# Grouping the state update and the 64-row steps of an mLSTM and feed-forward kernel

## The chip, the cores and the metric

The kernel runs on one core of a Trainium2 chip. The metric is the device time of one execution in microseconds (us); less is better. The profiles come from the hardware profiler.

## The reference

Two blocks follow one another. The first is an mLSTM cell with 4 batches, 8 heads, 768 steps and head size 40. The second is a feed-forward layer on the 3072 tokens that come out, with width 320 and 2048 hidden units.

```python
for t in range(S):
    m_new = np.maximum(f_gate[:, :, t] + m, i_gate[:, :, t])
    f_stab = np.exp(f_gate[:, :, t] + m - m_new)
    i_stab = np.exp(i_gate[:, :, t] - m_new)
    m = m_new
    C = f_stab[..., None, None] * C + i_stab[..., None, None] * np.einsum('bhd,bhe->bhde', vt, kt)
    n = f_stab[..., None] * n + i_stab[..., None] * kt
    h_tilde = np.einsum('bhde,bhe->bhd', C, qt)
    denom = np.maximum(np.abs(np.einsum('bhd,bhd->bh', n, qt)[:, :, None]), 1.0)
    y[:, :, t] = h_tilde / denom / (1.0 + np.exp(-o_gate[:, :, t]))
x = y.transpose(0, 2, 1, 3).reshape(B * S, H * D)
h = x @ w_in
out = (h / (1.0 + np.exp(-1.702 * h))) @ w_out
```

## The kernel before

The sequence is cut into six windows of 128 steps, `w` = 0 to 5. Inside a window the recurrence is computed as attention: scores of q and k, weighted by the gates and masked, times v, plus what the state from earlier windows gives. Everything is float32; one matmul of the program is two matmuls (and two weight loads) in the profile. TensorE (PE) executes them in order. It is used in several array forms: all 128 rows and columns; two halves of 64 rows side by side (scores `p_s`, and the last 64 of the 320 inputs of the up-projection, `w_in_x`, L423); two halves of 64 columns side by side (`p_o`, `p_i`, and the state update `p_c`); and 32 rows for the decay product (L282).

A window goes through these stages.

- `gates(w)` on VectorE (DVE) computes the running gates. From window 1 on its `dec` is a 32-row operand, from which `columns` makes the decay of the states by a matmul with `half`.
- `attention(w)` is a list of eight steps: `columns`, then for step s the functions `seam` of batch s-3, `values` of batch s-2, `scores` of batch s-1 and `weights` of batch s. GpSimd (POOL) masks the weights (L329) and copies 64 columns of y (L372). `values` reads v (`v_st`, with a column of ones at its end) and the state.
- `up(w, j)` is the up-projection of the pairs j and j+1 of the 16 blocks of 128 hidden units, for all four batches at once: `full(j)` is 8 matmuls of 512 columns, `rest(j)` 4 of the 64-row form. Its order is full, rest, rest, full. `gelu` on ScalarE (ACT) takes the result out of PSUM.
- `carry(w, b)` makes the new states of batch b: POOL scales v into `vw` (L386) and multiplies the old state by its decay (L396), PE multiplies k by `vw` (L391), and DVE adds (L400; a copy, L402, in window 0). Carries 0 and 1 follow the first `up` of a window, carries 2 and 3 the second.
- `down` (window 0) and `down_fast` (windows 1 to 5) are the down-projection. The eight attention steps of the next window are spread between its blocks, at the places in `stops`. `hidden_sums` on DVE prepares operands for `down_fast`, and `weight_sums` does so once, in window 1.

Window 0 also converts the weights, which arrive as 64-bit numbers: `convert(n)` does piece n with two operations on ACT and four on DVE (L224 to L229). Pieces 3 and 4 are converted within the first `up` of window 0, pieces 18 and 19 between blocks of its down-projection, each ahead of the `transposes` of batch 2 and 3 of window 1 on DVE. `transposes` turns k and q (L294), and `scores` waits for it.

PSUM has two pools of four banks: `ps_m` for up- and down-projection, `ps_a` for all else. Loads and stores are issued by SyncE (SP) in the program's order; `spread` sends the gate rows, which `gates` has written to DRAM (`m_row`), to all 128 partitions.

Of the kernel before, what the change touches and what calls it, by code (L numbers as in the profile page):

```python
# [8 lines left out]
FP = mybir.dt.float32  # L9
# [25 lines left out]
def kernel(  # L35
# [156 lines left out]
        V.tensor_scalar(out=pick[j * BH:(j + 1) * BH, :], in0=ident[0:BH, 0:BH], scalar1=-1.0, scalar2=None,  # L192
                        op0=OP.mult)

    half = const.tile([BH, 2, 64], FP, name="half")
    par = const.tile([BH, 2], FP, name="par")
    pair = const.tile([BH, BH // 2], FP, name="pair")
    V.tensor_reduce(out=par, in_=ident[0:BH, 0:BH].rearrange("p (j two) -> p two j", two=2), axis=AX.X, op=OP.add)
    V.tensor_reduce(out=pair, in_=ident[0:BH, 0:BH].rearrange("p (j two) -> p j two", two=2), axis=AX.X, op=OP.add)
    V.tensor_copy(out=half, in_=par.unsqueeze(2).to_broadcast([BH, 2, 64]))  # L200
    for t in (k_st, q_st):
        G.memset(t[:, :, D:DP], 0.0)

# [28 lines left out]
    def gates(w):  # L232
        m = m_at[w]
        f_run = gate.tile([BH, L], FP, bufs=1, name="f_run")
        m_run = gate.tile([BH, L], FP, bufs=1, name="m_run")
        st = stacked[w] = gate.tile([3 * BH, L], FP, name="st")
        V.tensor_tensor_scan(out=f_run, data0=ones, data1=f_sb[w], initial=0.0, op0=OP.mult, op1=OP.add)
        a = st[0:BH, :]
        V.tensor_tensor(out=a, in0=i_sb[w], in1=f_run, op=OP.subtract)
        if w == 0:  # L240
            room = work.tile([L, H, D1], FP, tag="u", name="room").rearrange("p h d -> p (h d)")
            neg, part = room[0:BH, 0:L], room.bitcast(BF)[0:BH, 2 * L:3 * L]
            V.tensor_tensor(out=neg, in0=f_run, in1=i_sb[w], op=OP.subtract)
            for j in range(3):
                G.tensor_copy(out=part, in_=neg)
                G.tensor_copy(out=a3[j * BH:(j + 1) * BH, :], in_=part)
                if j < 2:
                    G.tensor_tensor(out=neg, in0=neg, in1=part, op=OP.subtract)
        V.tensor_tensor_scan(out=m_run, data0=ones, data1=a, initial=m, op0=OP.mult, op1=OP.max)
        if w == 0:  # L250

            room = work.tile([L, H, D1], FP, tag="u", name="room").rearrange("p h d -> p (h d)")
            left, part = room[0:BH, 0:L], room.bitcast(BF)[0:BH, 2 * L:3 * L]
            for j in range(3):
                rest = left if j else m_run
                V.tensor_copy(out=part, in_=rest)
                V.tensor_copy(out=m3[j * BH:(j + 1) * BH, :], in_=part)
                if j < 2:
                    V.tensor_tensor(out=left, in0=rest, in1=part, op=OP.subtract)
        else:  # L260
            m_row[w] = rows.tile([BH, L], FP, name="m_row")
            nc.sync.dma_start(out=m_row[w], in_=m_run)
        end = m_run[:, L - 1:L]
        if w + 1 < NW:
            m_at[w + 1] = gate.tile([BH, 1], FP, name="m_end")
            V.tensor_tensor(out=m_at[w + 1], in0=f_run[:, L - 1:L], in1=end, op=OP.add)

        V.tensor_scalar(out=st[BH:2 * BH, :], in0=m_run, scalar1=m, scalar2=None, op0=OP.subtract)
        V.tensor_scalar(out=st[2 * BH:3 * BH, :], in0=a, scalar1=end, scalar2=-1.0, op0=OP.subtract, op1=OP.mult)
        if 0 < w < NW - 1:  # L270
            dec[w] = gate.tile([BH, BH // 2], FP, name="dec")
            both = gate.tile([BH, 1], FP, name="both")
            V.tensor_tensor(out=both, in0=m, in1=end, op=OP.subtract)
            V.tensor_scalar(out=dec[w], in0=pair, scalar1=both, scalar2=None, op0=OP.mult)

    def columns(w):
        pt = ps_a.tile([L, 3 * BH + BH // 2], FP, tag="a", name="p_cols")
# [101 lines left out]
            T.transpose(px[:, c, :], ys[w, b][:, c * 128:(c + 1) * 128], ident)  # L379
        A.copy(out=xT[w][:, :, b, :], in_=px)  # L380

    def carry(w, b):
        hs = slice(b * H, (b + 1) * H)
        vw = work.tile([L, H, D1], FP, tag="vw", name="vw")
        e = cols[w][:, 2 * BH + b * H:2 * BH + (b + 1) * H].unsqueeze(2).to_broadcast([L, H, D1])
        G.tensor_tensor(out=vw, in0=v_st[:, hs, :], in1=e, op=OP.mult)  # L386
        pc = ps_a.tile([128, NP, D1], FP, tag="a", name="p_c")
        for p in range(NP):
            for i in range(2):
                h = 2 * p + i  # L390
                T.matmul(pc[i * 64:i * 64 + D, p, :], k_st[:, b * H + h, 0:D], vw[:, h, :], start=True, stop=True)  # L391
        ps = slice(b * NP, (b + 1) * NP)
        if w:
            d = cols[w][:, 3 * BH + b * NP:3 * BH + (b + 1) * NP].unsqueeze(2).to_broadcast([128, NP, 2 * D1])
            old = state[:, ps].rearrange("p j a b -> p j (a b)")
            G.tensor_tensor(out=old, in0=old, in1=d, op=OP.mult)  # L396
        for i in range(2):
            r = slice(i * 64, i * 64 + D)
            if w:
                V.tensor_tensor(out=state[r, ps, i, :], in0=pc[r], in1=state[r, ps, i, :], op=OP.add)  # L400
            else:
                V.tensor_copy(out=state[r, ps, i, :], in_=pc[r])  # L402


    def up(w, j, between=None):

        x = xT[w].rearrange("p c b t -> p c (b t)")
        ph = {}  # L410
        ts = slice(0, W)

        def full(j, first):
            for c in range(2):
                for i in range(2):
                    f = 2 * j + i
                    T.matmul(ph[j][i][:, ts], w_in_sb[:, c, f * 128:(f + 1) * 128], x[:, c, ts],  # L417
                             start=(first and c == 0), stop=(not first and c == 1))

        def rest(j, first):  # L420
            for i in range(2):
                r = slice(i * 64, i * 64 + 64)
                T.matmul(ph[j][i][:, ts], w_in_x[r, j, :], x[r, 2, ts], start=first, stop=not first)  # L423

        def gelu(j):
            g = gs[w, j] = gp.tile([128, 2, W], FP, tag="g", name="g")
            for i in range(2):
                A.activation(out=g[:, i, :], in_=ph[j][i], func=AF.Gelu_apprx_sigmoid)  # L428

        if between:  # L430
            for k in (j, j + 1):
                ph[k] = [ps_m.tile([128, W], FP, tag="m", name="p_h") for _ in range(2)]
            ts = slice(0, W // 2)
            full(j, True)
            between[0]()
            rest(j, False)
            rest(j + 1, True)
            between[1]()
            full(j + 1, False)
            between[2]()  # L440
            ts = slice(W // 2, W)
        for j, first in ((j, True), (j + 1, False)):
            if j not in ph:
                ph[j] = [ps_m.tile([128, W], FP, tag="m", name="p_h") for _ in range(2)]
            if first:
                full(j, True)
            rest(j, not first)
            if not first:
                full(j, False)
            gelu(j)  # L450

    def down(w, b, n):
        if n == 0:
# [79 lines left out]
    def attention(w):  # L533
        steps = [[(columns, w)]]
        for s in range(B + 3):
            step = []
            for lag, f in ((3, seam), (2, values), (1, scores), (0, weights)):
                if 0 <= s - lag < B:
                    step.append((f, w, s - lag))
            steps.append(step)  # L540
        return steps

# [47 lines left out]
    def weights_in(n):  # L590
        done, ahead = beside.get(n, ((), ()))
        for p in done:
            convert(p)
        for p in ahead:
            fetch(p)

    for w in range(NW):
        more = w + 1 < NW
        for j in range(NF // 2):
            if j % 2 == 0:  # L600
                if w == 0 and j == 0:
                    up(w, j, (lambda: values(0, 2), lambda: values(0, 3),
                              lambda: (seam(0, 2), seam(0, 3), convert(3), convert(4))))
                    weights_in(0)
                else:
                    if w == 0:
                        weights_in(j // 2)
                    up(w, j)
            if j == 0 and more:
                load(w + 1, "o")  # L610
            if w == 0 and j == 0:
# [5 lines left out]
            if more:  # L617
                if w and j == 0:
                    gates(w + 1)
                if j == 4:  # L620
                    if w == 0:
                        load_blocks(1, 1)
                    load(w + 1, "v")
                    if w:
                        spread(w + 1)
                if j == (4 if w else 6):
                    load(w + 1, "k")
                if j < B:
                    carry(w, j)
                if w == 0 and j == 0:  # L630
                    G.memset(q_bl, 0.0)
                if w and 4 <= j < 6:
                    transposes(w + 1, 2 * j - 8)
                    transposes(w + 1, 2 * j - 7)
# [56 lines left out]
```

## Time and profile before

| | |
|---|---|
| median of 7 runs | 516.41 us (516.39 to 518.82) |
| profiled execution | 516.43 us, span 514.7 us |
| PE busy | 506.3 us, 98% of the span |
| DVE, ACT, POOL busy | 268.5, 169.2, 71.1 us |
| up-projection matmuls, 128 rows (L417) | 400, 175.6 us |
| up-projection matmuls, 64 rows (L423) | 200, 48.0 us |
| state matmuls p_c (L391) | 320, 8.1 us |
| POOL vw (L386), state decay (L396) | 20 of 0.829 us, 16 of 0.893 us (mean) |
| granted TensorE clock | 1.00 |

Busy time of an engine is the union of its instructions, so matmuls that overlap count once. A matmul's recorded length includes its way through the array (0.6 us for 512 columns); the pace is read from the starts. An engine's idle time costs something only where PE waits for it. In the timeline, rows of one kind that follow without a gap are merged into one.

### The profile page before, as it was taken

How to read it: one execution, taken by the hardware profiler on the slowest of the kernel's cores; microseconds unless marked ns; L12 is line 12 of the kernel's file. 1: busy time of each engine (PE TensorE's matmuls, PEld its weight loads, DVE VectorE, ACT ScalarE, POOL GpSimd, SP SyncE). 2: the span in 40 equal slices, each digit the busy share in tenths (PEclk: the TensorE clock that was granted, in tenths of full speed). 3: DMA queues.
4: the chain of work that ended last, by engine and by line, in shares of the span. 5: the costliest groups of instructions: out<-in, count | busy, mean ns of one | idle time of the engine just before them, and what ended most of it. 6: DMA issues, size and time to landing. Idle time of an engine off the chain costs nothing.

```text
span 514.7 us, 9527 instructions
## 1 busy us (share of the span) xinstructions
PE 506.3 (98%) x3838; PEld 351.3 (68%) x3838; DVE 268.5 (52%) x597; ACT 169.2 (33%) x373; POOL 71.1 (14%) x104
## 2 busy tenths in 40 slices
PE   8899999999999999999999999999999999999997
PEld 4774367774449996447999445999543899744797
DVE  6879984963865543175454146455137545203511
ACT  5557675303128202215421122720212730122100
POOL 7231000112301102200212200110120111000000
PEclk9999999999999999999999999999999999999999
DMA  9999789005897404686100495400485000000000
GB/s 148 180 302 293 118 222 184 5 33 80 103 254 81 59 3 78 124 165 69 28 14 20 83 244 62 44 27 1 79 210 56 0 29 1 27 0 0 1 27 25
DMA packets 175691, 44.80 MB, mean 87 GB/s; under 512 B 164352, under 2 KB 170528, under 8 KB 175648
## 3 DMA queue, kind: packets, MB, share of 16 engines
q1 hardware_dynamic: 175648, 44.21, 45.7%
q8 instruction: 30, 0.49, 0.4%
q14 instruction: 13, 0.11, 0.1%
HBM read 40.17 MB, written 4.01 MB: 86 GB/s over the span
## 4 chain that ended last, share of the span: by engine, by line
PE 94%; DVE 2%; POOL 1%; ACT 1%; issue 1%; DVEq 0%; POOLq 0%
PE p_h L417 33%; PE p_out L511 30%; PE p_h L423 9%; PE p_out L457 7%; PE p_o L350 5%; PE p_s L339 4%; PE p_i L356 2%; PE p_c L391 1%; PE p_x L379 1%; DVE wt L341 0%; ACT xT L380 0%; POOL k_bl L555 0%; DVE pick L192 0%; PE p_cols L282 0%; POOL state L554 0%
## 5 line engine op out<-in xcount | busy, mean ns | idle before, releaser
L417 PE MATMUL p_h<-xT,w_in_sb 128*128 128x512 f32 (+1 forms) x400 | 175.6, 585 | 1.2 <-ACT xT L380 1.2
L417 PEld LDWEIGHTS p_h<-xT,w_in_sb 128*128 128x128 f32 x400 | 72.7, 190 | 90.4 <-issue 86.9
L428 ACT ACTIVATE g<-p_h 128x512 f32<-128x512 f32 x96 | 54.6, 596 | 155.8 <-PE p_h L423 91.1
L511 PE MATMUL p_out<-w_out_sb,g 128*128 128x160 f32 x480 | 71.3, 302 | 0.0
L511 PEld LDWEIGHTS p_out<-w_out_sb,g 128*128 128x128 f32 x480 | 66.8, 190 | 3.7 <-issue 2.4
L516 DVE TENSOR_TENSOR o_sb<-o_sb,p_out 128x160 f32<-128x160 f32 x70 | 21.5, 319 | 72.9 <-PE p_out L511 72.3
L380 ACT COPY xT<-p_x 128x384 f32<-128x384 f32 x24 | 11.4, 480 | 134.8 <-PE p_x L379 134.8
L329 POOL TENSOR_SCALAR_AFFINE_SELECT wt<-wt 128x1024 f32<-128x1024 f32 x24 | 26.6, 1108 | 174.7 <-ACT wt L326 142.8
L326 ACT ACTIVATE wt<-wt,cols 128x128 f32<-128x128 f32 x160 | 48.3, 390 | 0.0
L423 PE MATMUL p_h<-xT,w_in_x 64*128 64x512 f32 (+1 forms) x200 | 48.0, 598 | 0.2 <-DVE w_in_x L229 0.2
L511 PE MATMUL p_out<-t,s 128*128 128x160 f32 x320 | 47.5, 301 | 0.0
L511 PEld LDWEIGHTS p_out<-t,s 128*128 128x128 f32 x320 | 44.3, 190 | 0.6
L495 DVE TENSOR_TENSOR s<-g 128x512 f32<-128x512 f32 x20 | 13.9, 693 | 54.0 <-ACT g L428 54.0
L400 DVE TENSOR_TENSOR state<-p_c,state 40x164 f32<-40x164 f32 x32 | 10.4, 326 | 53.9 <-PE p_c L391 53.5
L423 PEld LDWEIGHTS p_h<-xT,w_in_x 64*128 64x128 f32 x200 | 17.2, 186 | 29.0 <-issue 27.4
L457 PE MATMUL p_out<-w_out_sb,g 128*128 128x320 f32 x128 | 36.2, 437 | 0.0
L341 DVE TENSOR_TENSOR wt<-p_s,wt 128x512 f32<-128x512 f32 x48 | 30.8, 684 | 8.3 <-PE p_s L339 5.5
L457 PEld LDWEIGHTS p_out<-w_out_sb,g 128*128 128x128 f32 x128 | 23.8, 190 | 10.1 <-issue 0.5
L350 PEld LDWEIGHTS p_o<-v_st,wt 128*64 128x64 f32 x768 | 24.3, 138 | 6.4 <-issue 4.7
L350 PE MATMUL p_o<-v_st,wt 128*64 128x41 f32 x768 | 27.2, 231 | 1.4 <-DVE wt L341 1.4
L339 PE MATMUL p_s<-qT,kT 40*128 40x128 f32 x384 | 27.9, 285 | 0.5 <-DVE wt L341 0.4
L339 PEld LDWEIGHTS p_s<-qT,kT 40*128 40x128 f32 x384 | 23.3, 187 | 3.9 <-issue 1.3
(114 smaller groups left out, 507.9 us busy)
## 6 DMA issues: line engine op xcount, KB each, us to landing
wt<-m_row SPq DMA_DIRECT2D x20, 512.0 KB, 6.4
bits<-in_moe_w_in_dram SPq DMA_DIRECT2D x8, 512.0 KB, 5.6
out_dram<-o_sb SPq DMA_DIRECT2D x24, 160.0 KB, 1.8
eo<-in_o_gate_dram SPq DMA_DIRECT2D x5, 640.0 KB, 5.7
v_st<-in_v_dram SPq DMA_DIRECT2D x5, 640.0 KB, 5.9
k_st<-in_k_dram SPq DMA_DIRECT2D x5, 640.0 KB, 8.2
bits<-in_moe_w_out_dram SPq DMA_DIRECT2D x8, 320.0 KB, 4.3
k_bl<-in_k_dram SPq DMA_DIRECT2D x40, 64.0 KB, 2.7
```

What stands on the lines that cost most here:

```text
L326: A.activation(out=x[:, h, :], in_=x[:, h, :], func=AF.Exp, scale=-1.0, bias=cols[w][:, b * H + h:b * H + h + 1])
L329: G.affine_select(out=x, in_=x, compare_op=OP.is_ge, fill=0.0, base=0, pattern=[[0, H], [1, L]], channel_multiplier=-1)
L339: T.matmul(pw[i][:, p, :], kT[w, b][r, p, :], qT[w, b][r, p, :], start=True, stop=True)
L341: V.tensor_tensor(out=wt[w, b][:, :, i, :], in0=pw[i], in1=wt[w, b][:, :, i, :], op=OP.mult)
L350: T.matmul(po[t, h, :], wt[w, b][:, p, i, t], v_st[:, b * H + h, :], start=True, stop=True)
L417: T.matmul(ph[j][i][:, ts], w_in_sb[:, c, f * 128:(f + 1) * 128], x[:, c, ts], start=(first and c == 0), stop=(not first and c == 1))
L423: T.matmul(ph[j][i][:, ts], w_in_x[r, j, :], x[r, 2, ts], start=first, stop=not first)
L428: A.activation(out=g[:, i, :], in_=ph[j][i], func=AF.Gelu_apprx_sigmoid)
L457: T.matmul(po, gs[w, f // 2][:, f % 2, b * L:(b + 1) * L], w_out_sb[:, f, :], start=(f == 0), stop=(f == NF - 1))
L495: V.tensor_tensor(out=s1, in0=a10, in1=a11, op=OP.add)
L511: T.matmul(po, a(f), b[:, f, :], start=(f == 0), stop=(f == NH - 1))
L516: V.tensor_tensor(out=dst, in0=x, in1=po, op=OP.add)
```

## The change

- `carry(w, b)` is split. `scale(w, b)` scales v in place and multiplies the old state by its decay, both on POOL; for windows 1 to 4 it is issued within the attention steps, behind `values` of the same batch, and for window 0 behind the first `up`. The new `carry(w)` does the matmuls and additions of all four batches in two PSUM tiles of `ps_a`, and sets the ones of `v_st` again on POOL.
- `up` takes n pairs. With n = 4 (windows 1 to 5) the order is full, full, rest, rest, rest, rest, full, full; the last two pairs take banks of `ps_a`. Where states are made, `carry(w)` stands between the first fulls and the rests. In window 0, n stays 2 and `carry(0)` is in the second `up`.
- The decay product has 96 rows: `dec` and `half` are padded with zeros, set once at the start.

```diff
-    half = const.tile([BH, 2, 64], FP, name="half")
+    half = const.tile([3 * BH, 2, 64], FP, name="half")
+    dec_in = const.tile([3 * BH, 2, BH // 2], FP, name="dec_in")
+    V.memset(half, 0.0)
+    V.memset(dec_in, 0.0)
...
-    V.tensor_copy(out=half, in_=par.unsqueeze(2).to_broadcast([BH, 2, 64]))
+    V.tensor_copy(out=half[0:BH], in_=par.unsqueeze(2).to_broadcast([BH, 2, 64]))
...
-            dec[w] = gate.tile([BH, BH // 2], FP, name="dec")
+            dec[w] = dec_in[:, w % 2, :]
...
-            V.tensor_scalar(out=dec[w], in0=pair, scalar1=both, scalar2=None, op0=OP.mult)
+            V.tensor_scalar(out=dec[w][0:BH, :], in0=pair, scalar1=both, scalar2=None, op0=OP.mult)
...
-    def carry(w, b):
...
+    def scale(w, b):
+        x = v_st[:, b * H:(b + 1) * H, :]
         e = cols[w][:, 2 * BH + b * H:2 * BH + (b + 1) * H].unsqueeze(2).to_broadcast([L, H, D1])
-        G.tensor_tensor(out=vw, in0=v_st[:, hs, :], in1=e, op=OP.mult)
+        G.tensor_tensor(out=x, in0=x, in1=e, op=OP.mult)
         if w:
             d = cols[w][:, 3 * BH + b * NP:3 * BH + (b + 1) * NP].unsqueeze(2).to_broadcast([128, NP, 2 * D1])
+            old = state[:, b * NP:(b + 1) * NP].rearrange("p j a b -> p j (a b)")
             G.tensor_tensor(out=old, in0=old, in1=d, op=OP.mult)
+
+    def carry(w):
+        for c in range(2):
+            ps = slice(c * 2 * NP, (c + 1) * 2 * NP)
+            pc = ps_a.tile([128, 2 * NP, D1], FP, tag="a", name="p_c")
+            for p in range(2 * NP):
+                for i in range(2):
+                    h = c * 4 * NP + 2 * p + i
+                    T.matmul(pc[i * 64:i * 64 + D, p, :], k_st[:, h, 0:D], v_st[:, h, :], start=True, stop=True)
+            for i in range(2):
+                r = slice(i * 64, i * 64 + D)
+                if w:
+                    V.tensor_tensor(out=state[r, ps, i, :], in0=pc[r], in1=state[r, ps, i, :], op=OP.add)
+                else:
+                    V.tensor_copy(out=state[r, ps, i, :], in_=pc[r])
+        G.memset(v_st[:, :, D:D1], 1.0)
...
-    def up(w, j, between=None):
+    def up(w, j, n, between=None, states=False):
+        begin, end = range(j, j + n // 2), range(j + n // 2, j + n)
...
-        for j, first in ((j, True), (j + 1, False)):
...
+        for k in begin:
+            if k not in ph:
+                take(k, ps_m, "m")
+            full(k, True)
+        if states:
+            carry(w)
+        for k in begin:
+            rest(k, False)
+            gelu(k)
+        for k in end:
+            if k not in ph:
+                take(k, *((ps_m, "m") if n == 2 else (ps_a, "a")))
+            rest(k, True)
+        for k in end:
+            full(k, False)
+            gelu(k)
...
+            if 0 <= s - 2 < B and w + 1 < NW:
+                step.append((scale, w, s - 2))
...
+                if w:
+                    if j % 4 == 0:
+                        up(w, j, 4, states=more and j == 0)
+                elif j == 0:
...
+                    for b in range(B):
+                        scale(0, b)
...
+                    up(w, j, 2, states=(j == 2))
...
-                if j < B:
-                    carry(w, j)
```

More of the change, by code (lines that the diff above doesn't have):

```diff
@@ L380, in seam @@
         A.copy(out=xT[w][:, :, b, :], in_=px)
-    def carry(w, b):
-        hs = slice(b * H, (b + 1) * H)
-        vw = work.tile([L, H, D1], FP, tag="vw", name="vw")
+    def scale(w, b):
+        x = v_st[:, b * H:(b + 1) * H, :]
         e = cols[w][:, 2 * BH + b * H:2 * BH + (b + 1) * H].unsqueeze(2).to_broadcast([L, H, D1])
[L386 to L392, printed above, removed]
+        G.tensor_tensor(out=x, in0=x, in1=e, op=OP.mult)
@@ L393, in carry @@
         if w:
             d = cols[w][:, 3 * BH + b * NP:3 * BH + (b + 1) * NP].unsqueeze(2).to_broadcast([128, NP, 2 * D1])
-            old = state[:, ps].rearrange("p j a b -> p j (a b)")
+            old = state[:, b * NP:(b + 1) * NP].rearrange("p j a b -> p j (a b)")
             G.tensor_tensor(out=old, in0=old, in1=d, op=OP.mult)
[L397 to L402, printed above, removed]
@@ L409, in up, with take @@
+    def up(w, j, n, between=None, states=False):
         x = xT[w].rearrange("p c b t -> p c (b t)")
+        begin, end = range(j, j + n // 2), range(j + n // 2, j + n)
         ph = {}
         ts = slice(0, W)
+        def take(j, pool, tag):
+            ph[j] = [pool.tile([128, W], FP, tag=tag, name="p_h") for _ in range(2)]
         def full(j, first):
@@ L431, in up @@
             for k in (j, j + 1):
-                ph[k] = [ps_m.tile([128, W], FP, tag="m", name="p_h") for _ in range(2)]
+                take(k, ps_m, "m")
             ts = slice(0, W // 2)
@@ L441, in up @@
             ts = slice(W // 2, W)
-        for j, first in ((j, True), (j + 1, False)):
[L443 to L450, printed above, removed]
+        for k in begin:
+            if k not in ph:
+                take(k, ps_m, "m")
+            full(k, True)
[11 more added lines that the diff above has]
+            gelu(k)
     def down(w, b, n):
@@ L600 @@
             if j % 2 == 0:
-                if w == 0 and j == 0:
-                    up(w, j, (lambda: values(0, 2), lambda: values(0, 3),
-                              lambda: (seam(0, 2), seam(0, 3), convert(3), convert(4))))
+                if w:
+                    if j % 4 == 0:
+                        up(w, j, 4, states=more and j == 0)
+                elif j == 0:
+                    up(w, j, 2, (lambda: values(0, 2), lambda: values(0, 3),
+                                 lambda: (seam(0, 2), seam(0, 3), convert(3), convert(4))))
+                    for b in range(B):
+                        scale(0, b)
                     weights_in(0)
                 else:
-                    if w == 0:
-                        weights_in(j // 2)
-                    up(w, j)
+                    weights_in(j // 2)
+                    up(w, j, 2, states=(j == 2))
             if j == 0 and more:
```

## The prediction

> **What bounds the kernel now.** I read the page's busy shares and the chain first: they say whose time must shrink.
>
> ```profile
> PE 506.3 (98%) x3838; PEld 351.3 (68%) x3838; DVE 268.5 (52%) x597; ACT 169.2 (33%) x373; POOL 71.1 (14%) x104
> ...
> PE 94%; DVE 2%; POOL 1%; ACT 1%; issue 1%; DVEq 0%; POOLq 0%
> ```
>
> TensorE (PE) is the bound and hardly waits: a gain must come out of its own stream. Next came the timeline of PE in the up-projection of window 2 (columns: start us, length us, engine, line, operation, tiles, form, count). It shows what a change of array form costs.
>
> ```profile
> 202.87 1.99 PE L423 MATMUL p_h<-xT,w_in_x 64*128 64x512 f32 x8
> 204.79 3.70 PE L417 MATMUL p_h<-xT,w_in_sb 128*128 128x512 f32 x8
> 208.42 0.81 PE L391 MATMUL p_c<-vw,k_st 128*40 128x41 f32 x32
> 209.16 3.70 PE L417 MATMUL p_h<-xT,w_in_sb 128*128 128x512 f32 x8
> ```
>
> ```profile
> 224.63 7.13 PE L417 MATMUL p_h<-xT,w_in_sb 128*128 128x512 f32 x16
> 231.69 1.99 PE L423 MATMUL p_h<-xT,w_in_x 64*128 64x512 f32 x8
> ...
> 239.32 0.25 PE L278 MATMUL p_cols<-ident,st 96*128 96x96 f32 x1
> 239.50 0.39 PE L282 MATMUL p_cols<-dec,half 32*128 32x16 f32 x2
> 239.82 2.44 PE L511 MATMUL p_out<-t,s 128*128 128x160 f32 x16
> ```
>
> Subtract starts. A run of 8 full matmuls between two other forms takes 208.42 - 204.79 = 3.63, a run of 16 takes 7.06. The 8 more cost 3.43, 0.429 each, so each run pays 0.20 for its two borders. The single starts show where: the last matmul before a border is followed after 0.52 instead of 0.43 (0.094), the first after it holds the next back to 0.53 (0.104, a weight load that nothing covers). The run of 64-row matmuls (1.92 = 4 pairs x 0.429 + 0.20) pays the same. So a trip full - 64 rows - full costs 0.40. For the state matmuls (p_c, two array halves side by side, a pair each 0.038) the trip costs 0.094 + 0.037 of slow start, then 0.098 + 0.105: 0.334.
>
> **The change, part by part.** F is a full pair (8 matmuls), R its 64-row part, C state matmuls.
>
> *Up-blocks and states, windows 1 to 4.* Before: F R R F four times, C twice: 4 x 0.40 + 2 x 0.334 = 2.27. After: F F C R R R R F F, then F F R R R R F F. The first costs 0.131 into C, C to R, then 0.201 back; C to R is in no row, its nearest is p_i (column halves) to p_s (64-row form), whose starts lose 0.098 + 0.101 = 0.20. Bounds: 0.10, if only the gap at the border stays, and 0.40, if the border is paid twice. I take 0.20. Sum 0.53 + 0.40 = 0.93, a gain of 1.34; four windows 5.35.
>
> *Window 5 (no states).* Four trips become two: 0.80.
>
> *Window 0.* C, F R F, C (1.07) becomes F C R R F (0.53): 0.54. But C ahead of F2 was cover. The second half of F2 needs the weights of `convert(4)`, whose last DVE operation (L229) ended at 41.16. It needed them at 41.68; without C ahead it does at 40.94. POOL's scaling now lies earlier, beside `convert(3)` and with the 1.8 us memset of q_bl after it, so DVE should end near where it did: a wait of 0 to 0.8, taken as 0.25.
>
> *Decay product, 4 times.* From the 96-row transpose to the next p_out is 0.50 (239.32 to 239.82), and that p_out's second matmul is 0.104 late. The transpose itself follows a full p_out with no loss, so 96 rows is the full form. After: three steps at about 0.11, since nothing but a 128-column weight load (p_x, 0.109 apart) limits them. 0.60 - 0.33 = 0.27; 1.08 in all. If the padded product still changed form, 0.
>
> *Start.* Two DVE memsets come ahead of the gates, where DVE runs without a gap. By the memset of 128x64 (0.11) they take 0.16 and 0.08; bounds 0 and 0.25, I take 0.20.
>
> *POOL's products move* from the up-projection to the attention steps: 2 each step (0.735 each), queued behind the y copy and the mask of the same step; the next y copy and mask wait behind them, over 4 us later. At the end of `carry` a memset of v_st's ones (like L552, 0.15) waits for C, with POOL's next work far off. These rows show what POOL's products do to DVE beside them:
>
> ```profile
> 39.87 1.88 POOL L386 TENSOR_TENSOR vw<-v_st,cols 128x328 f32<-128x328 f32 x2 [3.38 <-PE p_c L391]
> ...
> 40.00 1.16 DVE L229 CUSTOM_DVE_ANT_0 w_in_sb<-bits,w_in_sb 128x1024 uint16<-128x1024 uint16 x1
> ...
> 41.08 0.96 DVE L224 TENSOR_SCALAR w_in_sb<-w_in_sb 128x512 f32<-128x512 f32 x1
> ```
>
> Undisturbed, those two DVE operations take 0.69 and 0.42: two products cost DVE 1.0. Now the place to which they move, the down-projection of window 0, where DVE converts weights:
>
> ```profile
> 91.74 1.09 POOL L329 TENSOR_SCALAR_AFFINE_SELECT wt<-wt 128x1024 f32<-128x1024 f32 x1
> 92.61 0.50 DVE L224 TENSOR_SCALAR w_out_sb<-w_out_sb 128x512 f32<-128x512 f32 x1
> ...
> 95.67 0.67 DVE L294 STREAM_TRANSPOSE qT<-q_bl 128x512 f32<-128x512 f32 x1
> 95.69 0.77 PE L356 MATMUL p_i<-state,qT 128*64 128x82 f32 x16
> 96.49 0.72 PE L339 MATMUL p_s<-qT,kT 40*128 40x128 f32 x8
> ```
>
> The products of batch 0 would start at 92.83, behind the mask, beside `convert(18)`; the transposes behind it end at 96.34, and p_s follows at 96.49: no slack. Batch 3's scores are as tight (qT ends 103.92, p_s starts 104.07). What DVE loses there, PE waits. By these rows 2 x 1.0 = 2.0. [...] I take the row. [...] In the down-projections of windows 1 to 3 the same products fall after L341 and beside output adds that read PSUM, with 2 us of slack (DVE's product done 255.53, p_o at 257.62): 0.
>
> *Other waits, costed at nothing.* The last two of the four pairs take ps_a banks, and R of the fourth needs those of C back: DVE's four adds of 128x328 size (L360: 0.50) need 2.0, begin at half of C, and PE comes there three R (0.86 each) and a border after C, 2.7: about 1 us of cover; without it, PE waits what exceeds it, four times. In windows 1 to 4 the gates' work on DVE, and with it the m_row DMA and the `spread` queued behind it on SP, comes some 8 us later; the rows are needed 30 us on. g of pair 4 comes later, but pairs 6 and 7 end as before, and DVE reaches their sums in time (0.7 after the last matmul, needed from 0.83).
>
> **Sum.** 5.35 + 0.80 + 1.08 + 0.54 - 0.25 - 0.20 - 2.0 = 5.3. The profiled execution took 516.43 (span 514.7, 1.7 around it), the median is 516.41: both give 511.1.
>
> **Rivals.** (a) Likeliest, 0.72: 511.1, itself 510.2 to 512.2 by the small bounds.
>
> (b) [...] 0.13.
>
> (c) [...] 0.10.
>
> (d) Slower: 64 state matmuls in one group outrun PE's sequencer. [...] Against it:
>
> ```profile
> L391 PEldq EVENT_SEMAPHORE  x10: 51/51/51, 36.3 to 372.7; - x10
> ```
>
> The last of these belongs to the second half of a C run that began at 372.66: the sequencer had got no further than 16 matmuls ahead, and the following 16 still ran at 19 ns. So the row speaks for 1.2 us for the group; 0.03 for this, and 0.02 for an unseen new wait of its size.
>
> (e) The 96-row product keeps its own form: 512.2, inside the range.
>
> **How the numbers follow.** About 0.3% (1.5 us) is what a measurement can tell: the line lies at 514.9. Cases (a), (b), (c) lie below: 0.94; 0.02 for a loss that just eats the gain; 0.04 for (d) and above. The range 509.0 to 513.0 holds (a), most of (b), some of (c).
>
> **What would show it.** Right: F runs of 16 and R runs of 16 in windows 1 to 5 (about 3.64 each R run), one C run of 64 at about 1.3, an up-projection of 36.5 instead of 37.8 us (199.34 to 237.15); p_cols to p_out 0.3; POOL products beside `convert(18)` and `(19)` and p_s of batches 2 and 3 of window 1 about 1 us late. Wrong: p_s on time, R of the fourth pair waiting for DVE's state adds, or C slower than 40 ns a pair.

## The result and the profile after

The changed kernel takes 511.62 us (median of 12 runs), the kernel before 516.4: ratio 0.9907, 95% interval 0.9893 to 0.9921. It is faster by 4.8 us where 5.3 were forecast. The profiled execution took 511.63, with a span of 509.9. Executions with a lower mean of the clock granted to TensorE were longer (513.18 at 0.997, 515.48 at 0.99), so medians are compared, and stages that ran at 1.00.

The page of the kernel after, with busy shares and the chain:

```profile
PE 498.7 (98%) x3838; PEld 352.5 (69%) x3838; DVE 265.1 (52%) x579; ACT 168.1 (33%) x373; POOL 68.1 (13%) x109
...
PE 90%; DVE 7%; POOL 1%; issue 1%; ACT 1%; DVEq 0%; POOLq 0%
```

PE is still the bound, with as many matmuls and 7.6 us less of busy time (506.3 to 498.7). But DVE now holds 7% of the chain instead of 2%: a part of what PE gained it spends waiting. The timeline of PE in window 1 after (start us, us, engine, line, operation, tiles, form, count; in brackets the idle time ahead and what ended it) shows the gain:

```profile
119.15 7.13 PE L429 MATMUL p_h<-xT,w_in_sb 128*128 128x512 f32 x16 [0.57 <-ACT xT L384]
126.22 1.43 PE L403 MATMUL p_c<-v_st,k_st 128*40 128x41 f32 x64
127.57 3.70 PE L435 MATMUL p_h<-xT,w_in_x 64*128 64x512 f32 x16
131.21 14.00 PE L429 MATMUL p_h<-xT,w_in_sb 128*128 128x512 f32 x32
145.14 3.70 PE L435 MATMUL p_h<-xT,w_in_x 64*128 64x512 f32 x16
148.77 7.13 PE L429 MATMUL p_h<-xT,w_in_sb 128*128 128x512 f32 x16
...
157.92 0.25 PE L282 MATMUL p_cols<-ident,st 96*128 96x96 f32 x1
158.00 0.32 PE L286 MATMUL p_cols<-dec_in,half 96*128 96x16 f32 x2
158.17 2.01 PE L530 MATMUL p_out<-t,s 128*128 128x160 f32 x13
```

Read starts: 16 matmuls of the 64-row form take 131.21 - 127.57 = 3.64, the 64 state matmuls 127.57 - 126.22 = 1.35 with their borders, and from the transpose (L282) to p_out is 0.25 where it was 0.50. The two runs of full matmuls in the middle have become one of 32, since the block that ends with F is followed by one that begins with F.

Window by window, from the first full matmul of an up-projection to the first p_out, and from there to the next up-projection, in the two profiled executions:

| stage | before | after | difference |
|---|---|---|---|
| to the first up-projection | 25.69 | 25.82 | +0.13 |
| up, window 0 | 42.27 | 43.08 | +0.81 |
| down, window 0 | 49.16 | 50.26 | +1.10 |
| up, window 1 | 37.91 | 36.59 | -1.32 |
| up, windows 2 to 4, each | 37.81 | 36.49 | -1.32 |
| down, windows 1 to 3, each | 44.31 | 44.05 | -0.26 |
| up, window 5 | 35.93 | 35.13 | -0.80 |

The down-projections of windows 4 and 5, which have neither decay nor moved product, stay at 43.83 and 33.58. The differences add up to the difference of the spans, -4.83 (514.72 to 509.89). Window 0 loses twice. First, in its up-projection (timeline of PE, then of DVE, then of POOL, all of the kernel after):

```profile
39.94 1.96 PE L429 MATMUL p_h<-xT,w_in_sb 128*128 128x512 f32 x4 [0.58 <-DVE w_in_sb L233]
42.20 1.98 PE L429 MATMUL p_h<-xT,w_in_sb 128*128 128x512 f32 x4 [0.31 <-DVE w_in_sb L233]
```

```profile
34.91 0.71 DVE L228 TENSOR_SCALAR w_in_sb<-w_in_sb 128x512 f32<-128x512 f32 x1 [2.02 <-ACT w_in_sb L224]
35.66 2.58 DVE L229 TENSOR_SCALAR w_in_sb<-w_in_sb 128x512 uint32<-128x512 uint32 x1
...
41.45 0.69 DVE L233 CUSTOM_DVE_ANT_0 w_in_sb<-bits,w_in_sb 128x1024 uint16<-128x1024 uint16 x1
```

```profile
33.22 3.00 POOL L390 TENSOR_TENSOR v_st<-v_st,cols 128x328 f32<-128x328 f32 x4
36.16 1.80 POOL L654 MEMSET q_bl<- 128x2048 f32 x1
```

An operation of `convert(3)` that takes 0.43 elsewhere lasts 2.58: it ends 0.28 after the memset ends (35.66 + 2.58 = 38.24; 36.16 + 1.80 = 37.96). Both halves of the second pair's weights are late (the second is ready at 41.45 + 0.69 = 42.14), and PE waits for both. By the starts the two groups of four come 0.75 and 0.47 late, and the slower step behind each adds 0.18 in all. Second, in the down-projection (timeline of PE, of the kernel after and then of batch 3 in the kernel before):

```profile
96.37 0.77 PE L360 MATMUL p_i<-state,qT 128*64 128x82 f32 x16
97.99 1.16 PE L343 MATMUL p_s<-qT,kT 40*128 40x128 f32 x16 [0.84 <-DVE qT L298]
...
104.86 0.77 PE L360 MATMUL p_i<-state,qT 128*64 128x82 f32 x16
106.11 1.16 PE L343 MATMUL p_s<-qT,kT 40*128 40x128 f32 x16 [0.47 <-DVE qT L298]
```

```profile
103.37 0.77 PE L356 MATMUL p_i<-state,qT 128*64 128x82 f32 x16
104.07 1.16 PE L339 MATMUL p_s<-qT,kT 40*128 40x128 f32 x16
```

From p_i to p_s is 1.62 and 1.25, where it was 0.80 and 0.70: 1.37 lost. With the 0.26 that the decay product gains in this stage, that is its +1.10.

### The profile page after: what moved, and what is told of

The parts are those of the page before. It is cut to its first block, busy times and chain, and to the rows that moved or that the text cites. A ratio compares the mean times of both kernels' runs of the same rounds, so it can differ in the third digit from the quotient of the medians.

```text
span 509.9 us, 9498 instructions
## 1 busy us (share of the span) xinstructions
PE 498.7 (98%) x3838; PEld 352.5 (69%) x3838; DVE 265.1 (52%) x579; ACT 168.1 (33%) x373; POOL 68.1 (13%) x109
## 4 chain that ended last, share of the span: by engine, by line
PE 90%; DVE 7%; POOL 1%; issue 1%; ACT 1%; DVEq 0%; POOLq 0%
PE p_h L429 32%; PE p_out L530 31%; PE p_h L435 8%; PE p_out L476 5%; PE p_o L354 4%; PE p_s L343 4%; PE p_i L360 2%; PE p_c L403 1%; PE p_x L383 1%; DVE wt L345 1%; DVE w_in_sb L229 1%; DVE w_out_sb L231 0%; DVE w_in_sb L231 0%; DVE w_in_sb L228 0%; ACT xT L384 0%
## 5 line engine op out<-in xcount | busy, mean ns | idle before, releaser
L429 PE MATMUL p_h<-xT,w_in_sb 128*128 128x512 f32 (+1 forms) x400 | 170.7, 580 | 2.1 <-ACT xT L384 1.2
L429 PEld LDWEIGHTS p_h<-xT,w_in_sb 128*128 128x128 f32 x400 | 74.2, 190 | 93.1 <-issue 88.4
L440 ACT ACTIVATE g<-p_h 128x512 f32<-128x512 f32 x96 | 53.5, 599 | 151.6 <-PE p_h L435 85.3
L435 PE MATMUL p_h<-xT,w_in_x 64*128 64x512 f32 (+1 forms) x200 | 45.3, 588 | 0.2 <-DVE w_in_x L233 0.2
L364 DVE TENSOR_TENSOR u<-p_i,cols 128x328 f32<-128x328 f32 x20 | 9.9, 496 | 28.5 <-PE p_i L360 28.5
```

## The experiments

Executions of several of these kernels lie at two times some 1.4 us apart (experiments 6 and 7 give the likely reason), so single windows of the profiles decide where medians are close.

**1. Blocks of two pairs in windows 1 to 5.**

```diff
-                    if j % 4 == 0:
-                        up(w, j, 4, states=more and j == 0)
+                    up(w, j, 2, states=more and j == 0)
```

> The changed kernel with up-blocks of two pairs in windows 1 to 5 (states still in the middle of the first). Theory (array-form borders of 0.20 us each): two more trips of 0.40 in each of five windows, 4.0 us above the changed kernel: 511.6 + 4.0 = 515.6; up-projection of window 2 at 37.29 instead of 36.49. Rival (the gain comes from moving POOL's products and from one state group, not from the grouping of the 64-row steps): within 1 us of the changed kernel, up to 512.6.

Measured: 515.53. The up-projection of window 2 is 37.28, of window 5 35.93, as before the change. The grouping of the 64-row steps alone is worth 4.0 us, as the theory says; the rival falls.

**2. Products of window 1 later.**

```diff
-            if 0 <= s - 2 < B and w + 1 < NW:
+            if 0 <= s - 2 < B and 1 < w < NW - 1:
...
         if w == 0:
+            for b in range(B):
+                scale(1, b)
             load_gates(2)
```

> The changed kernel with POOL's eight products of window 1 issued behind its whole attention, at the end of window 0's down-projection, not beside the conversion of pieces 18 and 19. Theory (POOL and DVE exclude each other there): p_s of batches 2 and 3 no longer wait for qT, 1.37 us less: 510.25. Rival (the wait is for something else, such as the transposes' DMA or the order of DVE): no change, 511.6.

Measured: 510.18. The timeline of PE of this kernel has both scores on time:

```profile
96.29 0.77 PE L360 MATMUL p_i<-state,qT 128*64 128x82 f32 x16
97.09 1.16 PE L343 MATMUL p_s<-qT,kT 40*128 40x128 f32 x16
...
103.97 0.77 PE L360 MATMUL p_i<-state,qT 128*64 128x82 f32 x16
104.67 1.16 PE L343 MATMUL p_s<-qT,kT 40*128 40x128 f32 x16
```

The down-projection of window 0 is 48.90 instead of 50.26; all else stays. Nothing but the place of POOL's products was changed, so the two waits are theirs.

**3. Two products added to the kernel before**, at the place to which the change moves its own, for batches 0 and 1 of window 1.

```diff
+    def products(w, b):
+        e = cols[w][:, 2 * BH + b * H:2 * BH + (b + 1) * H].unsqueeze(2).to_broadcast([L, H, D1])
+        for _ in range(2):
+            G.tensor_tensor(out=extra, in0=v_st[:, b * H:(b + 1) * H, :], in1=e, op=OP.mult)
...
+            if w == 1 and 0 <= s - 2 < 2:
+                step.append((products, w, s - 2))
```

> The kernel before, with two more POOL products (v times a gate column, into a tile that nobody reads) behind the values of batches 0 and 1 of window 1, where the change puts its own. Theory: DVE loses 0.8 in each, PE waits for qT twice, 1.4 us above the kernel before: 517.8. Rival (products beside the conversion cost PE nothing): 516.4.

Measured: 517.79 against 516.41; ratio 1.002, interval 1.0008 to 1.0031. The down-projection of window 0 grows from 49.16 to 50.53. Timelines of POOL and DVE of this kernel:

```profile
92.80 1.78 POOL L537 TENSOR_TENSOR extra<-v_st,cols 128x328 f32<-128x328 f32 x2
```

```profile
93.14 0.84 DVE L226 TENSOR_SCALAR w_out_sb<-w_out_sb 128x512 uint32<-128x512 uint32 x1
94.01 1.10 DVE L228 SCALAR_TENSOR_TENSOR w_out_sb<-bits,w_out_sb 128x512 uint32<-128x512 uint32 x1
```

Alone these two take 0.43 and 0.69. Each product costs DVE 0.41; of the 1.64 for all four, 1.37 reach PE. Experiments 2 and 3 show the same loss from both sides, 1.36 and 1.37.

**4. The memset of q_bl behind convert(4).**

```diff
+    mark = const.tile([128, 1], FP, name="mark")
...
+                    G.tensor_copy(out=mark, in_=w_in_sb[:, 1, 1023:1024])
                     G.memset(q_bl, 0.0)
```

> The changed kernel with the memset of q_bl on POOL held back until convert(4) has ended, by a one-column copy that reads its result. Theory: the DVE operation that lasted 2.58 us behind a product and the memset ends 1.8 us sooner, both waits of the second pair in window 0 (0.65 and 0.54) go: 1.1 us less, 510.5. Rival (the four products alone are enough to make DVE late): a gain of 0.3 us or less, 511.3.

Measured: 510.43. Timelines of DVE and POOL of this kernel:

```profile
39.45 0.84 DVE L230 TENSOR_SCALAR w_in_sb<-w_in_sb 128x512 uint32<-128x512 uint32 x1
```

```profile
37.00 3.01 POOL L391 TENSOR_TENSOR v_st<-v_st,cols 128x328 f32<-128x328 f32 x4
...
44.38 1.81 POOL L656 MEMSET q_bl<- 128x2048 f32 x1
```

The four products lie where they were, 2.45 ahead of the operation (2.44 in the kernel after). It lasts 0.84, and PE does not wait. From the first up-projection matmul behind the wait for xT to the first state matmul is 46.68 - 38.34 = 8.34, where the kernel after has 44.12 - 34.37 = 9.75: 1.41 less. (The whole stage is 1.65 shorter, at 41.43; the other 0.24 lies ahead of this stretch and isn't the memset's.) So the memset behind the products is what made PE wait, not the products alone.

**5. The decay product on 32 rows again**, with `half` and `dec_in` of 32 rows and without the two memsets.

```diff
-    half = const.tile([3 * BH, 2, 64], FP, name="half")
-    dec_in = const.tile([3 * BH, 2, BH // 2], FP, name="dec_in")
-    V.memset(half, 0.0)
-    V.memset(dec_in, 0.0)
+    half = const.tile([BH, 2, 64], FP, name="half")
+    dec_in = const.tile([BH, 2, BH // 2], FP, name="dec_in")
```

> The changed kernel with the decay product on 32 rows again, and without the two memsets at the start. Theory: four trips of 0.26 back (44.31 instead of 44.05 from the first p_out of window 1 to the next up-projection), 1.05 us in all, less 0.13 at the start: 512.5. Rival (the padded product is slower by itself and wins nothing): 511.5 or less.

Measured: 511.14, a miss by 1.4, and on the rival's side. The windows tell why. The down-projections of windows 0 to 3 grow by 0.26 to 0.28 each, 1.07 in all, as the theory has it. But the up-projection of window 0 fell from 43.08 to 41.75. A change that has nothing to do with that stage took its waits away.

**6. The same, with the zeros still written at the start.**

```diff
-            T.matmul(pt[:, 3 * BH:n], half.rearrange("p a b -> p (a b)"), dec[w], start=True, stop=True)
+            T.matmul(pt[:, 3 * BH:n], half[0:BH].rearrange("p a b -> p (a b)"), dec[w][0:BH, :], start=True, stop=True)
```

> The changed kernel with a 32-row decay product, but with the zeros still written at the start, so that DVE and POOL meet at the same moment in window 0. [...] Rival (something in the 32-row product itself relieves window 0): 511.2.

Measured: 511.44; the up-projection of window 0 is 41.67. My theory was that the start decides: with the zeros written there the two waits of window 0 come back, 512.7. It falls in this form: with the same start the waits are gone too. But the rival doesn't hold either, as the timelines of DVE and POOL of this kernel show:

```profile
35.65 0.84 DVE L229 TENSOR_SCALAR w_in_sb<-w_in_sb 128x512 uint32<-128x512 uint32 x1
36.53 0.69 DVE L231 SCALAR_TENSOR_TENSOR w_in_sb<-bits,w_in_sb 128x512 uint32<-128x512 uint32 x1
```

```profile
33.21 3.00 POOL L390 TENSOR_TENSOR v_st<-v_st,cols 128x328 f32<-128x328 f32 x4
36.16 2.08 POOL L654 MEMSET q_bl<- 128x2048 f32 x1
```

All stands where it stood in the kernel after, to some 3 ns: DVE's operation starts at 35.652 here and 35.655 there, in both 0.357 after the fourth product. The last product ends at 36.21, when both DVE's operation and the memset (36.16) have begun. Here DVE's operation ends first, after 0.84, and the memset lasts 2.08 instead of 1.80; there the memset ends first, after 1.80, and the operation lasts 2.58. Runs without a profile lie at the same two times, all at a granted clock of 0.999 or more. Of the kernel after, one of twelve took 510.24; in experiment 1, two of thirteen took 514.13 and 514.17 where the median is 515.53. In experiments 5 and 6, three of four runs are fast, and the fourth lies 1.4 above them (512.54 and 512.68). So the 32-row kernels seem to lose here too, only more seldom; why, no run shows. That these runs met the other order was not profiled.

**7. Only the start repaired**, `half` and `dec_in` written and filled just ahead of `gates(1)`.

```diff
-    V.memset(half, 0.0)
-    V.memset(dec_in, 0.0)
-    V.tensor_copy(out=half[0:BH], in_=par.unsqueeze(2).to_broadcast([BH, 2, 64]))
...
             if w == 0 and j == 0:
+                V.memset(half, 0.0)
+                V.memset(dec_in, 0.0)
+                V.tensor_copy(out=half[0:BH], in_=par.unsqueeze(2).to_broadcast([BH, 2, 64]))
                 gates(1)
```

> The changed kernel with only the start repaired: zeros and filling of half and dec_in moved to just ahead of gates(1), 0.3 us off DVE's chain at the start. [...]

My theory was that the distance in time between DVE and POOL alone decides which of the two ends first: 511.3 with the memset first and the second operation of `convert(3)` at 2.6, or 510.0 with that operation at 0.84. If the two waits of the second pair had another cause, time and length would not go together. Measured: 510.81, with runs from 509.87 to 513.71: both times occur (511.36, and 509.87 and 510.26), and the kernel alone doesn't fix which. In the profiled execution, 513.71, the operation lasted 2.58 and PE waited for it in two places, so length and wait go together; the other runs have no profile. The operation began 0.358 after the fourth product, as in experiment 6, where it came out the other way. So the distance in time between DVE and POOL, as far as a trace resolves it, does not decide the order, and the theory isn't confirmed in that part.

**8. States behind the first block of four pairs.**

```diff
                         up(w, j, 4)
+                        if more and j == 0:
+                            carry(w)
```

> The changed kernel with the state matmuls behind the first block of four pairs of windows 1 to 4, not between its full and 64-row steps. Theory: two borders more less one shared, 0.40 + 0.334 instead of 0.53 in four windows: 0.8 us above the changed kernel, 512.4. Rival (the place inside costs, because the fourth pair waits for the banks of the states): at or below 511.6.

Measured: 512.25 (four runs: 511.60, 511.61, 512.89 and 514.09, so that the median lies between the two times). The profile, of the run of 512.89, separates two parts: the up-projections of windows 1 to 4 are 0.20 longer each, as the two borders say, and the down-projection of window 1 is 0.61 longer. There the late states push back all that follows on DVE in that window, `weight_sums` among it, until a sum for the second product is late:

```profile
160.48 0.81 PE L530 MATMUL p_out<-t,s 128*128 128x160 f32 x4 [0.34 <-DVE s L515]
```

The place inside the block is thus worth its 0.8. The fourth pair does not wait for the banks of the states: in the kernel after, the 16 matmuls of the 64-row form follow one another without a gap.

**9. All three repairs** (experiments 2, 4 and 7 together).

> The changed kernel with three repairs of window 0: POOL's products of window 1 behind its attention, the memset of q_bl behind convert(4), and the zeros and the filling of half and dec_in moved from the start to just ahead of gates(1). Theory: 1.37 + 1.1 + some 0.2 less than the changed kernel, 508.9. Rival (the waits share one cause, so that the repairs don't add, or the waits come back at the next weights): 510 or more.

Measured: 508.61, ratio 0.9866 (0.9819 to 0.9914) to the kernel before, the fastest of all but for experiment 11, from which it can't be told apart. Start 25.43, up-projection of window 0 41.74, down-projection 48.90: the repairs add, and no other wait takes their place. The memset now holds back the next piece's first DVE operation (2.04 instead of 0.42), for which PE doesn't wait. It beats both kernels.

**10. A block of four in window 0 as well**, on top of the repairs.

```diff
...
+                elif j == 4:
+                    weights_in(2)
+                    weights_in(3)
+                    up(w, j, 4)
```

> The same three repairs, and in window 0 the last four pairs as one block of four too, with the conversions of pieces 9 to 14 ahead of it. Theory: one trip of 0.40 less, 508.5. Rival (ACT has six conversions, 7 us, ahead of the first gelu of the block, and the block waits for its banks): slower than the repairs alone.

Measured: 513.2 (nine runs, 510.90 to 515.69). The up-projection wins its 0.41 (41.33), but the down-projection is 53.48 instead of 48.90, 4.58 more. The rival's mechanism was not it either: the block did not wait for banks. The timelines of PE and SP show what was late:

```profile
83.11 1.16 PE L341 MATMUL p_s<-qT,kT 40*128 40x128 f32 x16 [2.67 <-DVE qT L296]
84.21 6.26 PE L474 MATMUL p_out<-w_out_sb,g 128*128 128x320 f32 x16
```

```profile
61.82 8.43 SPq L157 DMA_DIRECT2D bits<-in_moe_w_out_dram  x10
70.34 9.72 SPq L114 DMA_DIRECT2D q_bl<-in_q_dram  x16
```

`weights_in(3)` also issues the loads of pieces 18 and 19, and in this order they stand ahead of q's blocks in SP's queue, which began at 65.88 in the kernel before. The wait is not all of it. The 16 p_out matmuls behind it take 6.19 to the next start instead of 4.51, since the granted clock was 0.50 there (84.5 to 87.0). That is 1.68 of the 4.58; p_s itself comes 2.90 later than in experiment 9, counted from the transpose of that stage (L280).

**11. The same, with those loads at j = 6.**

```diff
-                    weights_in(3)
+                    for p in (12, 13, 14):
+                        convert(p)
                     up(w, j, 4)
+                else:
+                    for p in (18, 19):
+                        fetch(p)
```

> The three repairs and the block of four in window 0, now with the loads of pieces 18 and 19 behind the loads of q and k and not ahead of them. Theory (the block itself saves one trip of 0.41, and what it lost in the down-projection of window 0, 4.6 us, came from those loads holding SP's queue ahead of q's blocks, for which qT and p_s waited): 508.2. Rival (DVE and ACT, which convert six pieces ahead of the block, are late by themselves): over 510.

Measured: 508.57. Of the 4.58 us, 3.86 are gone, so the queue was their cause. In the profiled execution, at 509.07 the slowest of four, what the block wins (0.40) is more than spent in the down-projection (49.62 instead of 48.90), where the first p_s still waits 0.48 for qT. The other three took 508.50 to 508.62. No gain over experiment 9.

## Why the prediction was right, and where not

- *Up-blocks and states*: 1.34 a window forecast, 1.32 measured, and 0.80 for window 5. The border that no row showed, from the states to the 64-row form, costs 0.10 + 0.105 (single starts), as taken from p_i to p_s. Experiments 1 and 8 give 4.0 for the grouping and 0.8 for the place of the states.
- *Decay product*: 0.27 forecast, 0.26 measured, and experiment 5 gives it back. With 96 rows the product starts 0.086 after the transpose instead of 0.177, so no border is paid ahead of it; the second p_out behind it still comes 0.083 late, where it was 0.104.
- *Start*: 0.20 forecast, 0.13 measured.
- *POOL's products in the down-projection of window 0*: the place, the waiting instructions and the cause were right, the size was 2.0 and is 1.37. By the row, two products cost DVE 1.0; here they cost 0.82 (experiment 3). And for batch 3 not all of that reached PE (0.55): before the change DVE had idled 0.17 ahead of L360, which took up a part. No cost at all would have been wrong.
- *Up-projection of window 0*: this is the step that failed. The sum had 0.54 gained and a wait of 0.25, at most 0.8; measured is a loss of 0.81, that is 1.35 of waits. "DVE should end near where it did" does not hold: `convert(4)` ended at 42.14 instead of 41.16, and PE waited for both halves of the weights, not only for the second. The memset comes right behind the last product, and when it ends first, DVE's operation lasts past the end of both: 2.58 instead of 0.84. My rows had shown what POOL's products do to DVE, and none what the memset does. The kernel before had shown it (timelines of POOL and DVE):

```profile
33.82 1.80 POOL L631 MEMSET q_bl<- 128x2048 f32 x1
```

```profile
34.86 1.05 DVE L224 TENSOR_SCALAR w_in_sb<-w_in_sb 128x512 f32<-128x512 f32 x1 [2.04 <-ACT w_in_sb L220]
```

  This DVE operation, 0.42 alone, lasts until 0.29 after the memset's end, as the one of 2.58 does (0.28). Where DVE's operation ends first (experiment 6) the stage takes 41.67, 0.60 less than before the change, so the gain of 0.54 was sound.
- *Rival (d), a slower group of state matmuls*: it did not come true. 64 of them take 1.35 with their borders, 0.038 a pair to the end, or 19 ns a matmul.
- *Waits costed at nothing* stayed so: the fourth pair finds its banks, `spread` and the sums are in time. In experiment 8, states that come later in window 1 are enough to lose that.

The forecast of 511.1 for 511.62 is thus right by its mechanism in windows 1 to 5 and in the down-projection of window 0, and wrong in the up-projection of window 0. Two terms of window 0 erred, one by +0.63 and one by -1.10, and in part cancel; which of DVE's operation and the memset ends first moves a run by another 1.4. That the total came so close is in part luck.

## What to carry to other kernels

Where TensorE never waits, read starts and not lengths (here a matmul of 512 columns is recorded with 0.59 us, and the next starts after 0.43). In this kernel a run of the full or the 64-row form, of 8 matmuls, 16 or 32, cost 0.20 us at its two borders, so sorting matmuls by form, as far as the PSUM banks at hand went, was worth 4.0 us. When an operation leaves its old place, look at what it will run beside: POOL work that was free beside matmuls cost PE 1.4 us beside DVE's conversion of weights, and moving it again gave all of it back. What stood ahead of a stage may have been its cover: with the states gone from there, the weights' conversion, once held up, decided when the second pair could go on.

## What was not expected of the hardware

Two executions in which POOL and DVE reach the same point within 3 ns of each other differ by 1.4 us in this stage: once DVE's operation ends first (0.84) and the memset lasts 2.08, once the memset ends first (1.80) and DVE's operation lasts 2.58. What decides the order no run here shows. The kernels that leave this meeting in PE's path show two times 1.4 us apart. Holding the memset back by a one-column copy took it out of that path: in experiment 9 it meets a DVE operation for which PE doesn't wait.
